# K of two units leaves PSUM by ScalarE instead of VectorE, in a fused infini-attention and token-mixer kernel

## Chip, cores, metric

One core of a Trainium2 chip. The metric is the device time of the core in microseconds (us); smaller is better. TensorE ("PE" in the profile) does the matmuls; their results land in PSUM, in eight banks, 0 to 7. VectorE ("DVE") and ScalarE ("ACT") take them out of PSUM into SBUF, the on-chip memory for everything else, and GpSimd ("POOL") applies the causal mask there.

## The reference, cut to what matters

```python
xn = layernorm(x)                               # x: 1 x 2048 x 1024
out = x + A(xn, wq, wk, wv, wo, beta) + B(xn, w1, b1, w2, b2)

def A(x, ...):                                  # 32 heads of 32, 4 segments of 512 tokens
    phi = lambda t: where(t > 0, t + 1.0, exp(t))
    M, z = 0, 0
    for s in range(4):
        qs, ks, vs = ...                        # projections of this segment
        p = softmax(qs @ ks.T * scale + causal_mask)
        a_dot = p @ vs
        a_mem = (phi(qs) @ M) / (phi(qs) @ z + 1e-06)
        outs.append(g * a_mem + (1.0 - g) * a_dot)
        M, z = M + phi(ks).T @ vs, z + sum(phi(ks))
    return concat(outs) @ wo

def B(x, ...):                                  # mixes tokens: two matmuls with gelu between
    ...
```

## The kernel before, the parts that matter

The mixer B comes first; attention begins near 374 us, with the projections, and near 388 us with the logits. Attention is cut into 32 **units**: unit u is a group of four heads in segment u // 8. While unit u's logits are made, dense jobs (eight matmuls of 512 columns each, into PSUM bank 6 or 7 by turns) project Q and K of unit u + 2, project V and apply wo. K of units 0 to 15 is projected here and leaves PSUM by a VectorE cast; K of later units is loaded from memory, where an earlier part of the kernel has put it.

```python
def q_job(self, u):                     # ends in: ScalarE copies the bank to qT (line 1253)
    ...
def k_job(self, u):
    def end(b):
        fw, k = self.fw, u % 3
        fw.op("dve", lambda e: e.tensor_copy(self.kT[k][:], self.bank(b)),        # line 1262
              reads=[self.R_bank[b]], writes=[self.R_kT[k]])
        if u // N_GRP < N_SEG - 1:
            self.exps.append((1, self.kT[k], self.R_kT[k], u))   # exp(K), later, on ScalarE
    return self.proj_job(self.wk_ring, u, end)
```

The weighted values of a unit are made in three parts. Parts 0 and 2 share bank 4, part 1 has bank 5; VectorE takes each out by an addition into `ost`. So part 2 can't start before the addition of part 0 is done:

```python
def weigh(self, u, part):
    ...
    b = 4 + part % 2
    ...                                         # matmuls into bank b
        fw.op("dve", lambda e: e.tensor_tensor(dst, src, eps, op=ALU.add),        # line 1418
              reads=[self.R_bank[b], self.R_eps], writes=[self.R_ost[o][part]])
```

The order in which a unit's work is given out (cut; `dense(n)` is n matmuls of the waiting jobs; `self.side` is VectorE work that is slipped in between them):

```python
for u in range(N_UNIT):
    self.jobs.extend(self.unit_jobs(u))         # ..., Q of u + 2, K of u + 2 (last)
    self.dense(cuts[0]);  self.logits(u, 0)     # banks 0 to 3, then Exp on ScalarE, mask on GpSimd
    self.dense(cuts[1])
    self.weigh(u - 1, 0);  self.dense(cuts[2], False)
    self.weigh(u - 1, 1);  self.dense(cuts[3], False)
    self.weigh(u - 1, 2)
    ...                                         # side: combine (u - 1), phi of Q, then:
    if u + 1 < N_UNIT:
        self.side.append(lambda u=u: (self.phi_k(u + 1), self.k_transpose(u + 1)))
    self.dense(cuts[4]);  self.logits(u, 1)
    ...                                         # even u: logits step 2; then the rest of the jobs
```

Thus the end of round 11 puts into VectorE's queue, in this order, phi of K of unit 12 (the last of the side work), the cast of K of unit 13 (the last job), and, from the next round, the addition of part 0 of unit 11. Round 13 does the same two units later.

## Time and profile before

| | before |
|---|---|
| time, 3 runs | 652.3 us median (652.26 to 652.78) |
| TensorE busy | 645.9 us, 99% of the 650.5 us span |
| K's casts on VectorE | 16, 688 ns each |
| first Q matmul of unit 13 to part 2 of unit 11 ("stretch A") | 477.19 to 483.91: 6.72 us |
| first Q matmul of unit 15 to part 2 of unit 13 ("stretch B") | 496.45 to 503.18: 6.73 us |
| from there to the start of VectorE's last addition to the output ("rest") | to 648.30: 145.12 us |

A run's time varies by some tenths of a microsecond from its start-up and its loads, long before the changed instructions. The stretches begin and end within the trace of one run, so they leave that out. They follow TensorE, which is never long idle; between the end of A and the start of B lie 12.52 to 12.55 us in every kernel here.

The groups of instructions by line, for the two ways of taking a 512-column bank out of PSUM (line, engine, operation, output from input, shapes, count; then busy us and mean ns of one; then idle time before and its releaser):

```profile
L1253 ACT ACTIVATE qT<-ps_all 128x512 bf16<-128x512 f32 x32 | 19.0, 594 | 23.3 <-PE ps_all L199 23.3
L1262 DVE CAST kT<-ps_all 128x512 bf16<-128x512 f32 x16 | 11.0, 688 | 12.9 <-PE ps_all L199 12.9
```

The two engines need about the same time for it. VectorE's timeline at the end of round 11 has that queue (start and length in us, then engine, line and operation as above; in other lines a bracket at the end gives the engine's idle time just before and what ended it):

```profile
482.70 0.68 DVE L1262 CAST kT<-ps_all 128x512 bf16<-128x512 f32 x1
483.30 1.03 DVE L1418 TENSOR_TENSOR ost<-ps_all,eps 128x396 bf16<-128x396 f32 x2
```

The addition starts 0.60 us after the cast, though the cast is 0.68 long: neighbours on VectorE overlap a little. TensorE's timeline and the chain for the same moment are in the prediction.

### The profile page before, as it was taken

What the parts mean: (1) busy time and instruction counts of PE and PEld (TensorE: products, weight loads), DVE (VectorE), ACT (ScalarE), POOL (GpSimd) and SP (SyncE); (2) the same over time, 40 slices, a digit from 0 to 9 for tenths busy, and PEclk for the clock granted to TensorE, in tenths of its full rate; (3) what the DMA queues carried; (4) which work ended last, traced back from release to release, by engine and by line L of the source; (5) the groups of instructions that cost most, each with busy time, mean ns of one, the idle gap of its engine ahead of it and who ended that gap; (6) DMA issues with size and microseconds to landing.
All of it is one profiled execution on the core that took longest, in us unless ns stands there. A gap on an engine that the chain in (4) does not pass through costs nothing.

```text
span 650.5 us, 11182 instructions
## 1 busy us (share of the span) xinstructions
PE 645.9 (99%) x4611; PEld 303.6 (47%) x4611; DVE 433.7 (67%) x808; ACT 281.4 (43%) x305; POOL 154.2 (24%) x179
## 2 busy tenths in 40 slices
PE   9999999999999999999999999999999999999998
PEld 3444444444444444444444444444544454445544
DVE  6975676665555664744638325767887888777896
ACT  7543232232210000111101047778767778889770
POOL 2500000000011220220202203343334444554440
PEclk9999999999999999999999999999999999999999
DMA  9804233242498947538262957979654677435434
GB/s 303 216 0 130 65 107 88 64 116 79 127 261 193 238 120 210 157 102 231 79 208 96 263 130 177 184 168 227 134 135 98 155 165 139 112 98 128 105 94 139
DMA packets 190123, 95.00 MB, mean 146 GB/s; under 512 B 108664, under 2 KB 176248, under 8 KB 190072
## 3 DMA queue, kind: packets, MB, share of 16 engines
q1 hardware_dynamic: 189928, 94.25, 57.2%
q8 instruction: 36, 0.59, 0.4%
q14 instruction: 15, 0.12, 0.1%
q10 hardware_dynamic: 144, 0.03, 0.0%
HBM read 69.23 MB, written 11.53 MB: 124 GB/s over the span
## 4 chain that ended last, share of the span: by engine, by line
PE 94%; DVE 3%; ACT 2%; issue 1%; DMA 0%; POOL 0%; DVEq 0%
PE ps_all L199 94%; ACT pT L1364 1%; DVE prod L1465 1%; DVE ln_st L587 1%; DMA xin<-in_A_x_dram 0%; DVE h L627 0%; DVE ost L1418 0%; POOL ln_rs L611 0%; DVE mtmp L1230 0%; DVE kT L1262 0%; DVE fin L1307 0%; DVE mtmp L1228 0%; ACT qT L1253 0%; ACT vA L1293 0%; DVE ln_mv L590 0%
## 5 line engine op out<-in xcount | busy, mean ns | idle before, releaser
L1364 ACT ACTIVATE pT<-ps_all 128x2048 bf16<-128x2048 f32 x80 | 150.2, 1877 | 47.4 <-PE ps_all L199 46.9
L1368 POOL TENSOR_SCALAR_AFFINE_SELECT pT<-pT 128x512 bf16<-128x512 bf16 x128 | 105.6, 843 | 160.7 <-ACT pT L1364 160.7
L689 DVE TENSOR_TENSOR part<-ps_all,part 128x512 f32<-128x512 f32 x84 | 57.7, 690 | 108.2 <-PE ps_all L199 87.8
L1075 POOL TENSOR_TENSOR part<-part,stg 128x512 f32<-128x512 f32 x24 | 33.0, 1404 | 285.1 <-DVE part L689 285.1
L199 PE MATMUL ps_all<-wv,xnT 128*128 128x512 bf16 x256 | 68.5, 380 | 0.4 <-ACT qT L1253 0.2
L746 ACT ACTIVATE g<-part,b1c 128x512 f16<-128x512 f32 x36 | 26.0, 722 | 98.8 <-DVE part L689 98.8
L199 PE MATMUL ps_all<-xnT,wq 128*128 128x512 bf16 x256 | 66.4, 380 | 0.0
L199 PE MATMUL ps_all<-wo,oT 128*128 128x512 bf16 (+2 forms) x272 | 63.8, 367 | 0.0
L694 ACT ACTIVATE part<-ps_all 128x512 f32<-128x512 f32 x24 | 14.0, 596 | 101.1 <-PE ps_all L199 67.1
L1418 DVE TENSOR_TENSOR ost<-ps_all,eps 128x396 bf16<-128x396 f32 (+1 forms) x72 | 37.2, 522 | 28.5 <-PE ps_all L199 27.8
L199 PEld LDWEIGHTS ps_all<-vA,pT 128*128 128x128 bf16 x1280 | 45.7, 96 | 20.4 <-DVE ost L1418 1.7
L199 PE MATMUL ps_all<-g,sum 128*128 128x512 f16 x224 | 51.0, 379 | 0.0
L199 PE MATMUL ps_all<-g,w2s 128*128 128x512 f16 x224 | 51.0, 379 | 0.0
L199 PE MATMUL ps_all<-gT,sum 128*128 128x512 f16 x224 | 50.3, 379 | 0.0
L199 PE MATMUL ps_all<-vA,pT 128*128 128x33 bf16 x1280 | 48.5, 177 | 0.3 <-DVE ost L1418 0.3
L199 PE MATMUL ps_all<-h,sum 128*128 128x512 f16 x192 | 45.2, 379 | 0.0
L199 PE MATMUL ps_all<-h,w1s 128*128 128x512 f16 x192 | 44.9, 379 | 0.0
L199 PE MATMUL ps_all<-hT,sum 128*128 128x512 f16 x192 | 43.6, 379 | 0.0
L199 PEld LDWEIGHTS ps_all<-wo,oT 128*128 128x128 bf16 x272 | 23.9, 98 | 24.4 <-issue 3.7
L199 PEld LDWEIGHTS ps_all<-xnT,wq 128*128 128x128 bf16 x256 | 22.6, 97 | 25.4 <-issue 5.3
L199 PEld LDWEIGHTS ps_all<-g,sum 128*128 128x128 f16 x224 | 21.9, 98 | 26.4
L199 PEld LDWEIGHTS ps_all<-g,w2s 128*128 128x128 bf16 x224 | 21.9, 98 | 26.4
(118 smaller groups left out, 875.1 us busy)
## 6 DMA issues: line engine op xcount, KB each, us to landing
w2s<-in_B_w_dram SPq DMA_DIRECT2D x8, 1792.0 KB, 9.5
w1s<-in_B_w_dram SPq DMA_DIRECT2D x12, 1024.0 KB, 5.6
wq<-in_A_wq_dram SPq DMA_DIRECT2D x32, 256.0 KB, 3.3
xs<-in_A_x_dram SPq DMA_DIRECT2D x24, 256.0 KB, 3.4
stg<-in_A_x_dram SPq DMA_DIRECT2D x16, 256.0 KB, 2.9
out_dram<-stg SPq DMA_DIRECT2D x16, 256.0 KB, 3.9
wk<-in_A_wk_dram SPq DMA_DIRECT2D x16, 256.0 KB, 3.6
fin<-out_dram SPq DMA_DIRECT2D x16, 256.0 KB, 3.2
```

The costliest lines, as they stand in the source:

```text
L199: ins = self.nc.tensor.matmul(*args, **kwargs)
L587: fw.op("dve", lambda e: e.bn_stats(st[:, 6 * h:6 * h + 6], src[:, 512 * h:512 * h + 512]), reads=[self.R_xin[c]], writes=[R])
L689: self.fw.op("dve", lambda e: e.tensor_tensor(self.tmp[dst][:], self.bank(b), self.tmp[src][:], op=ALU.add), reads=[self.R_bank[b], self.R ...
L694: self.fw.op("act", lambda e: e.activation(self.tmp[dst][:], self.bank(b), ACT.Copy), reads=[self.R_bank[b]], writes=[self.R_tmp[dst]])
L746: self.fw.op("act", lambda e: e.activation(self.gB[f % 2][half][:, f // 2, :], src, ACT.Gelu_apprx_tanh, bias=self.b1c[:, f:f + 1], scale= ...
L1075: fw.op("pool", lambda e: e.tensor_tensor(self.tmp[t][:], self.tmp[t][:], self.stg[k][:, 512 * half:512 * half + 512], op=ALU.add), reads= ...
L1364: fw.op("act", lambda e: e.activation(dst, src, ACT.Exp, scale=SCALE), reads=self.R_bank[0:4], writes=[R[v % 2][kb] for v, kb, _ in blocks ...
L1368: fw.op("pool", lambda e: e.affine_select(d, d, pattern=[[0, 4], [1, P]], compare_op=ALU.is_ge, fill=0.0, base=0, channel_multiplier=-1), ...
L1418: fw.op("dve", lambda e: e.tensor_tensor(dst, src, eps, op=ALU.add), reads=[self.R_bank[b], self.R_eps], writes=[self.R_ost[o][part]])
L1465: fw.op("dve", lambda e: e.tensor_tensor(self.prod[:], ost[:, :, 0:D_HEAD], rec.unsqueeze(2).to_broadcast([P, 32, D_HEAD]), op=ALU.mult), ...
```

## The change

Intent: two of K's casts stand in front of an addition that TensorE waits for; ScalarE is idle at that moment, so it takes these two.

```diff
+    K_BY_ACT = (13, 15)
+
     def k_job(self, u):
         def end(b):
             fw, k = self.fw, u % 3
-            fw.op("dve", lambda e: e.tensor_copy(self.kT[k][:], self.bank(b)),
-                  reads=[self.R_bank[b]], writes=[self.R_kT[k]])
+            if u in self.K_BY_ACT:
+                fw.op("act", lambda e: e.activation(self.kT[k][:], self.bank(b), ACT.Copy),
+                      reads=[self.R_bank[b]], writes=[self.R_kT[k]])
+            else:
+                fw.op("dve", lambda e: e.tensor_copy(self.kT[k][:], self.bank(b)),
+                      reads=[self.R_bank[b]], writes=[self.R_kT[k]])
             if u // N_GRP < N_SEG - 1:
```

## The prediction

> **What bounds the kernel now.** I read the page's shares first, then the chain that ended last in order of time, then each engine's timeline around the two places that the change touches. The page says who carries the time:
>
> ```profile
> PE 645.9 (99%) x4611; PEld 303.6 (47%) x4611; DVE 433.7 (67%) x808; ACT 281.4 (43%) x305; POOL 154.2 (24%) x179
> PE 94%; DVE 3%; ACT 2%; issue 1%; DMA 0%; POOL 0%; DVEq 0%
> ```
>
> The first line is busy time by engine, the second the chain's shares. TensorE is busy 99% of the 650.5 us span and makes 94% of the chain. VectorE's 67% is therefore no bound on average; it can cost time only where TensorE stands still for it. A change on VectorE and ScalarE can win only what TensorE loses to waits. So I looked in the chain for K's eviction (line 1262) and found it twice (start in us, length in us, what):
>
> ```profile
> 482.09 0.69 DVE mtmp L1230
> 482.78 0.60 DVE kT L1262
> 483.38 0.49 DVE ost L1418
> 483.87 0.05 issue
> 483.91 11.86 PE ps_all L199 x127
> ...
> 501.36 0.69 DVE mtmp L1230
> 502.05 0.60 DVE kT L1262
> 502.65 0.49 DVE ost L1418
> 503.14 0.05 issue
> 503.18 42.96 PE ps_all L199 x485
> ```
>
> These are exactly units 13 and 15. K is evicted 16 times, in order of units, and the timeline of VectorE has the last three casts at 482.70, 490.87 and 501.96 us: units 13, 14, 15. Unit 14's isn't in the chain. Each time the chain passes through VectorE's queue: phi of K, then the cast of K, then the addition that takes part 0 of the weighted values (ost) out of bank 4, and only then TensorE may write part 2 into bank 4. The timeline of TensorE shows the hole:
>
> ```profile
> 482.75 0.22 PE L199 MATMUL ps_all<-MZbf,pqT 128*128 128x132 bf16 x1
> 483.17 0.59 PE L199 MATMUL ps_all<-wv,xnT 128*128 128x512 bf16 x2
> 483.91 0.57 PE L199 MATMUL ps_all<-vA,pT 128*128 128x33 bf16 x16 [0.16 <-DVE ost L1418]
> ...
> 502.00 1.02 PE L199 MATMUL ps_all<-wv,xnT 128*128 128x512 bf16 x4
> 503.18 0.57 PE L199 MATMUL ps_all<-vA,pT 128*128 128x33 bf16 x16 [0.16 <-DVE ost L1418]
> ```
>
> The bracket's 0.16 us counts from the modelled end of the last matmul, and matmuls overlap, so it understates the loss. I count starts instead. Where nothing waits, two matmuls of 512 columns take 0.43 us from start to start of what follows (482.32 to 482.75) and four take 0.86 (548.74 to 549.60, same operands, no wait). So TensorE wanted to start at 483.17 + 0.43 = 483.60 and at 502.00 + 0.86 = 502.86. It lost 483.91 - 483.60 = 0.31 us and 503.18 - 502.86 = 0.32 us, 0.63 us together, under 0.1% of the time. That is the whole prize; these are also the only two waits that the timeline marks before a matmul from 450 to 510 us.
>
> **What the Trainium skill says.** "VectorE: DVE Perf Modes", section on the TRN2 errata, gives a VectorE move from PSUM to SBUF 120 + N cycles at 0.96 GHz; for fp32 (no fast mode from PSUM) and N = 512 I work that out as 658 ns. The trace has 688 for the casts of line 1262, of which about 0.60 us is what each holds the queue (482.70 to 483.30). "ScalarE: Activation LUTs", section "What ACT_TABLE_LOAD costs", gives 186 ns + 0.833 ns per element with immediate scale and bias, 613 ns here, and an overlap of about 93 ns between instructions back to back. The same copy is in the trace as Q's eviction: 594 ns mean over 32, and an exponential starts 0.49 us after one (488.71 to 489.20), an overlap of 0.11. The same page, "Table sets: the hidden batching unit", says that copy is in every table set; the trace agrees: copies and exponentials alternate all through attention, and there are just two table loads (lines 506 and 1004), both earlier. "SBUF — State Buffer", "Who interferes with whom", says that a VectorE instruction with two SBUF inputs contends with a GpSimd one that reads SBUF. The trace fits: prod takes 1.22 us alone and 1.66 at 479.42, beside a POOL mask that runs from 479.25 to 481.57. The cast reads only PSUM, so taking it away should not alter that contention by itself.
>
> **The change part by part.** Removed: two of VectorE's 16 casts, 2 x 0.60 us of its queue. In the chain, both lie right in front of the addition that TensorE waits for. Without it, the addition follows phi of K at 482.70 instead of 483.30 (its input, part 0 in bank 4, was done by about 482.5) and ends at 483.30 + 0.57 - 0.60 = 483.27; TensorE wants the bank at 483.60. Margin 0.33 us, far above the 0.04 that TensorE needs after the addition. At unit 15: 501.96 + 0.57 = 502.53 against 502.86, the same margin. So 0.60 us less of queue buys not 0.60 but only the 0.31 and 0.32 that TensorE lost.
>
> Added: two copies on ScalarE, about 2 x 0.59 us. K's last matmul ends at 478.93 + 1.89 = 480.82. ScalarE is idle then:
>
> ```profile
> 479.12 0.60 ACT L1253 ACTIVATE qT<-ps_all 128x512 bf16<-128x512 f32 x1
> 481.19 1.88 ACT L1364 ACTIVATE pT<-ps_all 128x2048 bf16<-128x2048 f32 x1 [1.47 <-PE ps_all L199]
> ...
> 500.46 1.88 ACT L1364 ACTIVATE pT<-ps_all 128x2048 bf16<-128x2048 f32 x1 [1.47 <-PE ps_all L199]
> ```
>
> The copy runs from about 480.85, so the exponential behind it starts at 480.85 + 0.49 = 481.34 instead of 481.19: 0.15 us late. Behind it come the exponentials of Q and K and the V eviction, all 0.15 us later. Does that reach TensorE? The next logits rewrite banks 0 to 3 at 485.15 - 0.31 = 484.84, and this exponential ends near 483.22: 1.6 us to spare. The next exponential must start at 485.60 - 0.31 = 485.29, and ScalarE is free at 484.01 + 0.15 + 0.49 = 484.65. At unit 15 it is closer: free at 503.27 + 0.15 + 0.49 = 503.91, needed at 504.43 - 0.32 = 504.11, 0.20 us to spare. Hidden both times. K's exponential still finds its input: it starts 2.6 us after K's matmuls end, and now on the same engine.
>
> Moved: nothing in the order of TensorE's work, since the flag that puts VectorE's side work into the dense jobs stays as it is. The bank of K comes free about 1.9 us earlier, but its next user (wo at 484.62) came 1.2 us after the old cast's end at 483.38, so that buys nothing.
>
> Sum: 652.3 - 0.31 - 0.32 = 651.67 us.
>
> **The rivals.**
> 1. Another wait takes the place of this one, gain 0, 652.3 us. Part 2 needs, besides bank 4, the masked pT (POOL done at 481.57), pqT (VectorE done at 479.51), the transposed K (issued at 474.25, 3 us to land) and the state of a segment earlier. All are ready at least 2 us before 483.60, so I see nothing that could replace it.
> 2. ScalarE becomes the bound after unit 15, where only 0.20 us is spare. If its copy cost 0.3 us more than I think, the gain would halve: 652.0. Against it: ScalarE idles 0.57 to 1.47 us before the exponentials that wait for logits here.
> 3. The gain is lost again later. From 503.18 the chain is TensorE for 43 us; then near 550 and 580 it passes through ScalarE for some 5 us. Those stretches begin with logits from TensorE (550.84, 580.80, each released by PE), so they move along with it, and no DMA stands in the chain after the start. Had one paced it, 652.3.
> 4. The full 2 x 0.60 us of the chain's kT pieces is won: 651.1. The chain's length of a piece isn't its worth: TensorE has work up to 483.60 and 502.86 whatever VectorE does. I hold this for very unlikely, unless the earlier addition helps something that I don't see.
>
> **Range and chances.** The mechanism is marked in the chain, both margins are 0.3 us, and later parts hang on TensorE, so I take the full 0.63 us: 651.7 us. The three runs of before spread over 0.5 us (652.26 to 652.78), nearly as much as the effect, and rivals 1 to 3 lie within 0.6 us above. So 651.2 to 652.4. Two per cent is 13 us, eleven times the 1.2 us by which all of VectorE's removed work could shorten anything: within 2% 0.98, and 0.01 each for faster and slower.
>
> **What would show it right or wrong.** In the profile after: the two waits of TensorE on ost near 483.9 and 503.2 are gone, part 2 follows its dense matmuls after 0.43 and 0.86 us; kT has 14 casts on VectorE and two copies near 594 ns on ScalarE, each with the exponential 0.49 us behind its start; VectorE about 1.4 us less busy, ScalarE 1.2 more; work past 510 us comes 0.6 us earlier with the same spacing, to the end. I am wrong if part 2 still waits (for POOL, a DMA or the second addition), if a wait of TensorE on pT appears near 506, or if the 0.6 us at 510 us has shrunk by the end.

## More of the kernel before

The framework waits for every producer that an instruction needs, in the order in which they were found (this order matters in one experiment):

```python
def _waits(self, es, reads, writes, extra=()):
    need = {}
    ...
    for t in need.values():
        es.wait_tok(t)
```

## The result, and the profile after

After: 651.63 us median of 6 runs (651.51 to 652.13). Before, in the same rounds: 652.36 (652.19 to 652.78, 6 runs). Ratio 0.9989, 95% interval 0.9977 to 1.0002. Here and below, a ratio is the mean time of one kernel's runs over that of the other's of the same rounds, so it isn't quite the ratio of the medians quoted. The medians differ by 0.73 us, with 0.6 us of spread within each kernel. The interval includes 1, so the total times alone would not prove a gain. The trace does.

The page's shares after, to be held against the first two lines of the prediction:

```profile
PE 646.1 (99%) x4611; PEld 304.0 (47%) x4611; DVE 432.7 (67%) x806; ACT 282.3 (43%) x307; POOL 153.8 (24%) x179
PE 94%; ACT 2%; DMA 2%; DVE 1%; issue 0%; POOL 0%; SPq 0%; DVEq 0%
```

VectorE has two instructions fewer and ScalarE two more. VectorE's share of the chain fell from 3% to 1%: the chain no longer passes through its queue before 484 and 503, where it held about 6 us each time. The 2% of DMA come from the chain's early part, which in this run went through a load that ended later (below). TensorE's timeline at the two places, to be held against the prediction's:

```profile
483.67 0.59 PE L199 MATMUL ps_all<-wv,xnT 128*128 128x512 bf16 x2
484.10 0.56 PE L199 MATMUL ps_all<-vA,pT 128*128 128x33 bf16 x16
...
502.17 1.02 PE L199 MATMUL ps_all<-wv,xnT 128*128 128x512 bf16 x4
503.03 0.56 PE L199 MATMUL ps_all<-vA,pT 128*128 128x33 bf16 x16
```

Both brackets are gone. Part 2 follows its dense matmuls after 484.10 - 483.67 = 0.43 us and 503.03 - 502.17 = 0.86 us. VectorE's timeline shows why: phi of K is followed at once by the addition.

```profile
482.59 0.69 DVE L1230 SCALAR_TENSOR_TENSOR mtmp<-kT,mtmp 128x512 bf16<-128x512 bf16 x1
483.20 1.23 DVE L1424 TENSOR_TENSOR ost<-ps_all,eps 128x396 bf16<-128x396 f32 x2
```

ScalarE's timeline, at unit 13 and at unit 15:

```profile
481.36 0.60 ACT L1265 ACTIVATE kT<-ps_all 128x512 bf16<-128x512 f32 x1 [1.13 <-PE ps_all L199]
481.85 1.87 ACT L1370 ACTIVATE pT<-ps_all 128x2048 bf16<-128x2048 f32 x1
...
503.58 0.60 ACT L1299 ACTIVATE vA<-ps_all 128x512 bf16<-128x512 f32 x1
504.27 1.88 ACT L1370 ACTIVATE pT<-ps_all 128x2048 bf16<-128x2048 f32 x1
```

The new copy stands in what was idle time (1.13 us were still idle before it) and delays the exponential behind it, which starts 0.49 us after the copy. The debt is paid at the next gap: after the V copy at 503.58 ScalarE would be free at 503.58 + 0.49 = 504.07, and the exponential starts at 504.27 because its logits end at 504.22, not because ScalarE was late.

The chain of waits, in order of time, no longer goes through VectorE near 484 and 503:

```profile
170.29 8.25 DMA w2s<-in_B_w_dram
...
388.45 1.89 ACT pT L1370
390.38 155.60 PE ps_all L199 x1696
546.00 4.65 PE ps_all L199 x70
```

Before, it left TensorE twice in this range for VectorE (the prediction shows those lines); now TensorE runs from 390 to beyond 550 us with no other engine in between.

The stretches: A 6.41 us (was 6.72), B 6.40 (was 6.73), rest 145.11 (was 145.12). So 0.31 + 0.33 = 0.64 us were won, and none was lost afterwards.

One thing in this trace invites a wrong reading. The work past 510 us is only about 0.17 us earlier than before in absolute time (555.56 against 555.73 for the same V matmul). But the profiled run was the slowest of the six (652.13). It was already 0.31 us later than the one before at 159 us, and 0.50 later at the first VectorE sum behind the w2 load (178.57 against 178.07). The changed instructions run 300 us later; this is the load's and the start-up's spread between runs.

### The profile page after: what moved, and what is told of

It is laid out like the page before. It is cut to its first block, busy times and chain, and to the rows that moved or that the text cites. A ratio compares the mean times of both kernels' runs of the same rounds, so it can differ in the third digit from the quotient of the medians. Undisturbed runs are those within 1.5% of the kernel's fastest.

```text
span 650.4 us, 11182 instructions
## 1 busy us (share of the span) xinstructions
PE 646.1 (99%) x4611; PEld 304.0 (47%) x4611; DVE 432.7 (67%) x806; ACT 282.3 (43%) x307; POOL 153.8 (24%) x179
## 4 chain that ended last, share of the span: by engine, by line
PE 94%; ACT 2%; DMA 2%; DVE 1%; issue 0%; POOL 0%; SPq 0%; DVEq 0%
PE ps_all L199 94%; ACT pT L1370 1%; DMA w2s<-in_B_w_dram 1%; DMA xin<-in_A_x_dram 1%; DVE sum L648 0%; DVE ln_st L587 0%; DVE h L627 0%; ACT junk L600 0%; POOL ln_rs L611 0%; DVE part L689 0%; ACT junk L597 0%; ACT qT L1253 0%; ACT vA L1299 0%; DVE gT L663 0%; DVE ln_mv L609 0%
## 5 line engine op out<-in xcount | busy, mean ns | idle before, releaser
L199 PEld LDWEIGHTS ps_all<-gT,sum 128*128 128x128 f16 x224 | 21.9, 98 | 26.7 <-DVE gT L663 0.6
```

Of the source, the lines that this page charges most:

```text
L199: ins = self.nc.tensor.matmul(*args, **kwargs)
```

## The experiments

Theory: at two places TensorE stands 0.31 to 0.33 us before part 2, because the addition of part 0 stands behind a cast in VectorE's queue; what is won is exactly that standing time. Rivals: VectorE's total load counts (then any cast moved would do, and all of them would bring more); the copy on ScalarE costs something back; the gain is lost again later. Medians of the kernel before were 652.29, 652.26 and 652.38 us (9 runs each) in the three groups of runs (first to fourth, fifth to eighth, ninth to twelfth experiment).

| kernel | A | B | rest | time, median (range) | ratio [95%] |
|---|---|---|---|---|---|
| before | 6.72 | 6.73 | 145.12 | see above | 1 |
| the change | 6.41 | 6.40 | 145.11 | 651.63 (651.51 to 652.13) | 0.9989 [0.9977, 1.0002] |
| e1_only13 | 6.41 | 6.73 | 145.13 | 651.93 (651.81 to 652.44) | 0.9996 [0.9983, 1.0010] |
| e2_only15 | 6.73 | 6.40 | 145.13 | 652.12 (651.89 to 652.15) | 0.9996 [0.9984, 1.0009] |
| e3_even | 6.73 | 6.73 | 145.14 | 652.46 (652.24 to 653.42) | 1.0005 [0.9993, 1.0018] |
| e4_act_extra | 6.73 | 6.72 | 145.14 | 652.32 (652.25 to 652.57) | 1.0001 [0.9989, 1.0014] |
| e5_double | 7.46 | 7.45 | 145.14 | 653.77 (653.67 to 654.26) | 1.0024 [1.0012, 1.0037] |
| e6_phi_later | 6.40 | 6.40 | 145.78 | 652.25 (652.18 to 652.35) | 0.9999 [0.9986, 1.0013] |
| e7_all | 6.41 | 6.40 | 145.13 | 651.49 (651.46 to 651.67) | 0.9988 [0.9976, 1.0001] |
| e8_q_dve | 6.40 | 6.41 | 144.94 | 651.46 (651.28 to 651.61) | 0.9987 [0.9975, 1.0000] |
| e9_phi_later_first | 6.40 | 6.73 | 145.15 | 652.15 (651.88 to 652.36) | 0.9996 [0.9983, 1.0009] |
| e10_q_dve_order | 6.40 | 6.40 | 144.65 | 651.19 (651.14 to 651.41) | 0.9982 [0.9970, 0.9995] |
| e11_qv_dve_order | 6.41 | 6.40 | 144.78 | 651.35 (651.25 to 651.44) | 0.9984 [0.9970, 0.9997] |
| e12_after_again | 6.41 | 6.40 | 145.12 | 651.67 (651.65 to 651.93) | 0.9990 [0.9977, 1.0003] |

All in us; all correct; all within 2% of before. Each experiment has 5 runs. Between kernels that don't differ there, A and B repeat to 0.01 us and the rest to 0.04.

### e1_only13 and e2_only15: one unit at a time

```diff
-    K_BY_ACT = (13, 15)
+    K_BY_ACT = (13,)        # e1;  (15,) in e2
```

> K of unit 13 alone by ScalarE. I measure two stretches of TensorE in the profile: A from the first Q matmul of unit 13 to part 2 of unit 11 (6.72 us before, 6.41 after the change), B from the first Q matmul of unit 15 to part 2 of unit 13 (6.73 before, 6.40 after), and the rest from that part 2 to the last addition of the output (145.12 before, 145.11 after). Queue theory (only the addition behind the cast in VectorE's queue held TensorE): A 6.41, B 6.73, rest 145.1, time 0.3 us under before. Rival, total load of VectorE (any 0.6 us taken from it helps a little everywhere): A and B in between, rest shorter.

> K of unit 15 alone by ScalarE. Queue theory: A 6.72, B 6.40, rest 145.1, time 0.3 us under before; with e1 the two gains add to that of the change. Rival, the second wait exists only because the first put TensorE out of step: then B would be 6.40 in e1 too, and e2 would gain nothing.

Measured: each shortens its own stretch (6.41 and 6.40) and leaves the other at 6.73. From TensorE's timeline, in e1 the only wait marked at the two places:

```profile
502.74 0.57 PE L199 MATMUL ps_all<-vA,pT 128*128 128x33 bf16 x16 [0.16 <-DVE ost L1424]
```

and in e2:

```profile
484.06 0.58 PE L199 MATMUL ps_all<-vA,pT 128*128 128x33 bf16 x16 [0.16 <-DVE ost L1424]
```

So the two halves are independent and add up: 0.31 + 0.33.

### e3_even and e7_all: other casts

```diff
-    K_BY_ACT = (13, 15)
+    K_BY_ACT = (12, 14)              # e3;  tuple(range(2, 16)) in e7
```

> K of units 12 and 14 by ScalarE, 13 and 15 back on VectorE: as much moved, in units where VectorE is idle for over 2 us after the cast. Queue theory: A 6.72, B 6.73, rest 145.1, time as before within 0.15 us. Rival, load of VectorE, or ScalarE being the better engine for such a copy: about 0.6 us under before as in the change.

> K of units 2 to 15 by ScalarE. Queue theory: the other twelve casts held TensorE nowhere that the profile marks, so A 6.41, B 6.40 and the time is that of the change or up to 0.2 us off it, unless ScalarE comes late in the first segment, where it is busier. Load theory: 0.3 us for each cast moved, 4 us under before.

Measured: e3 takes as much load off VectorE as the change does, and wins nothing in any stretch (its time is 0.17 us above before's, with one outlier of 653.42). e7 takes off twelve casts more than the change, and its stretches are the change's to 0.02 us. VectorE's load as such isn't what counts; only the casts of units 13 and 15, with an addition behind them that TensorE waits for, bring anything.

### e4_act_extra: ScalarE's share of the change alone

In before, ScalarE copies the bank too, into a buffer that the later exponential overwrites; VectorE's cast stays:

```diff
     def end(b):
+        if u in (13, 15):
+            fw.op("act", lambda e: e.activation(self.etmp[2 * (u % 2) + 1][:], self.bank(b), ACT.Copy),
+                  reads=[self.R_bank[b]], writes=[self.R_etmp[2 * (u % 2) + 1]])
         fw.op("dve", lambda e: e.tensor_copy(self.kT[k][:], self.bank(b)), ...)
```

> The copies on ScalarE as an addition: K of units 13 and 15 is copied by ScalarE into a buffer that is overwritten right after, and VectorE's cast stays where it was. Queue theory: ScalarE's exponential after it starts 0.15 us later, TensorE does not see it: A 6.72, B 6.73, rest 145.1, time as before within 0.15 us. Rival, ScalarE's copy costs something that the change hides in its gain: A or B longer than before by up to 0.15 us, or a wait of TensorE on pT near 506 us.

Measured: 6.73, 6.72, 145.14, and 652.32 against 652.29. The two copies on ScalarE cost nothing here. TensorE is some 0.3 us late in this kernel anyway, so that a smaller cost could hide behind it; that the change itself has none is seen in its own stretches, where the full 0.31 and 0.33 are won and the rest is 145.11. Together they refute that ScalarE pays for the change.

### e5_double: the suspected cost twice

The cast of units 13 and 15 is given out twice, onto the same tile:

```diff
         fw.op("dve", lambda e: e.tensor_copy(self.kT[k][:], self.bank(b)), ...)
+        if u in (13, 15):
+            fw.op("dve", lambda e: e.tensor_copy(self.kT[k][:], self.bank(b)), ...)
```

> VectorE casts K of units 13 and 15 twice, one right behind the other. Queue theory: the addition comes 0.60 us later than before, so both holes grow by 0.60: A 7.32, B 7.33, rest 145.1, time 1.2 us over before. Rival, VectorE has slack and the hole comes from elsewhere (bank, POOL): A and B stay near 6.72.

Measured: A and B grew by 0.74 and 0.72, where I had put 0.60 each. VectorE's timeline, and TensorE's wait:

```profile
482.68 0.69 DVE L1262 CAST kT<-ps_all 128x512 bf16<-128x512 f32 x1
483.40 0.69 DVE L1265 CAST kT<-ps_all 128x512 bf16<-128x512 f32 x1
484.01 1.04 DVE L1421 TENSOR_TENSOR ost<-ps_all,eps 128x396 bf16<-128x396 f32 x2
```

```profile
484.63 0.58 PE L199 MATMUL ps_all<-vA,pT 128*128 128x33 bf16 x16 [0.89 <-DVE ost L1421]
```

The second cast starts 0.72 us after the first, 0.03 after its end, because it writes the same tile and waits on VectorE's own semaphore for it. The addition behind it depends on no cast and follows after 0.61, before the cast's end. So my doubling added a wait of 0.12 that the original doesn't have; the edit was not clean in that respect. The point stands: once the queue is later than TensorE wants, each further 0.72 us of it costs TensorE all of 0.72 (time +1.51 in the medians). The way back is not symmetric: taking 0.60 away wins only the 0.31 to 0.33 by which it was late.

### e6_phi_later: reorder the queue instead of moving work

K stays on VectorE everywhere. Phi of K of units 12 and 14, which stood in front of the casts, goes behind the addition of part 0:

```diff
+            if u - 1 in (11, 13):                 # right after self.weigh(u - 1, 0)
+                self.phi_k(u)
+                self.k_transpose(u)
...
-            if u + 1 < N_UNIT:
+            if u + 1 < N_UNIT and u not in (11, 13):
                 self.side.append(lambda u=u: (self.phi_k(u + 1), self.k_transpose(u + 1)))
```

> K stays on VectorE in all units; instead the phi of K of units 12 and 14 (0.93 us of VectorE's queue), which runs right before that cast, comes after the addition that takes part 0 of the weighted values out. Nothing is added on ScalarE. Queue theory: the addition comes 0.9 us earlier, A 6.41, B 6.40 as in the change, time 0.6 us under before. Rival, the gain came from K leaving its bank and being ready 2 us earlier by ScalarE: A 6.72, B 6.73, time as before.

Measured: both waits are gone (A 6.40, B 6.40), as expected, and still the time is before's: 652.25 against 652.26. (The rival, K's earlier release, isn't quite excluded by e6 alone, since VectorE's cast of unit 13 starts 0.94 us earlier too, at 481.76 instead of 482.70. But already before, the bank's next user came 1.24 us after the cast's end, so it had nothing to gain from it.) The rest has grown by 0.66. The expectation failed. The whole gain of both places is given back at one point, 5.7 us after part 2 of unit 13. TensorE there in e6:

```profile
508.23 1.25 PE L199 MATMUL ps_all<-wv,xnT 128*128 128x512 bf16 x5 [0.54 <-DVE fin L1307]
```

These matmuls take the bank that VectorE's addition `fin` (wo's result added to the output) empties. `prod` in front of it multiplies the weighted values by their scales. VectorE in e6:

```profile
505.91 1.65 DVE L1465 TENSOR_TENSOR prod<-ost,srec 128x1024 bf16<-128x1024 bf16 x1
507.49 0.68 DVE L1307 TENSOR_TENSOR fin<-ps_all,fin 128x512 bf16<-128x512 f32 x1
```

VectorE with the change:

```profile
506.22 1.22 DVE L1471 TENSOR_TENSOR prod<-ost,srec 128x1024 bf16<-128x1024 bf16 x1
507.36 0.68 DVE L1313 TENSOR_TENSOR fin<-ps_all,fin 128x512 bf16<-128x512 f32 x1
```

With the change, those matmuls start at 508.10, which is 5.07 us after part 2 (503.03); in e6 508.23 - 502.50 = 5.73. The 0.66 has two parts. First, the work was moved and not removed, so VectorE reaches its tail later: the update of the memory starts 503.97 - 502.50 = 1.47 us after part 2, against 504.27 - 503.03 = 1.24 with the change, 0.23 late. Second, `prod` takes 1.65 us instead of 1.22, 0.43 more. Beside it runs GpSimd's mask. First e6, then the change (each line is two masks):

```profile
505.69 2.38 POOL L1368 TENSOR_SCALAR_AFFINE_SELECT pT<-pT 128x512 bf16<-128x512 bf16 x2 [3.00 <-ACT pT L1364]
...
506.21 2.31 POOL L1374 TENSOR_SCALAR_AFFINE_SELECT pT<-pT 128x512 bf16<-128x512 bf16 x2 [2.86 <-ACT pT L1370]
```

With the change the first mask starts at 506.21, together with `prod` (506.22), and it is the mask that becomes long: 1.72 us, where one with no such neighbour takes 0.64. In e6 the first mask starts at 505.69, 0.22 us ahead of `prod`, and takes 0.81, so it still runs 0.59 us beside `prod`, which loses 0.43. Elsewhere `prod` loses 0.44 where the mask still runs 0.58 (before, 479.42), 0.31 where it runs 0.45 (after, 487.89) and 0.10 where it runs 0.24 (e9, 487.74). The Trainium skill, "SBUF — State Buffer", section "Who interferes with whom", has just this: a VectorE instruction with two SBUF inputs contends with a GpSimd instruction that reads SBUF, and the order of issue decides which of them is blocked. The trace agrees. TensorE and with it the logits, the exponential and the mask had come 0.53 us earlier, VectorE's `prod` only 0.31, and so their order flipped. 0.23 + 0.43 = 0.66. All of it reaches TensorE, because there is no slack at this point: with the change, too, the matmuls start only 0.06 us after `fin` ends (508.10 after 507.36 + 0.68 = 508.04), just as in e6 (508.23 after 508.17).

### e9_phi_later_first: the same at one place

If e6 failed because the moved work lies as a debt in front of a point without slack, then moving phi only at unit 12, where VectorE has 2.25 us idle after the unit to pay it, must win (edit against e6):

```diff
-            if u - 1 in (11, 13):
+            if u == 12:
...
-            if u + 1 < N_UNIT and u not in (11, 13):
+            if u + 1 < N_UNIT and u != 11:
```

> As e6, but only the phi of K of unit 12 comes later; that of unit 14 stays. In e6 both holes were gone (A and B 6.40) and the time came back at 508.23 us, where TensorE waited 0.54 us for VectorE's addition of the output (rest 145.78 instead of 145.11): after unit 13 VectorE has no idle time until then, while after unit 11 it idles 2.25 us. Debt theory: A 6.41, B 6.73, rest 145.1, time 0.3 us under before. Rival, late phi costs something by itself wherever it is: no gain, or the stretch from part 2 of unit 11 to the first Q matmul of unit 15 longer than 12.53.

Measured: A 6.40, B 6.73, rest 145.15, time 652.15 against 652.38. A's gain is kept. The debt belongs to the second place alone, where VectorE isn't idle between its tail and `fin`.

### e8_q_dve and e10_q_dve_order: the opposite move, later

From unit 16 on VectorE has no casts of K, and ScalarE is the busier helper. With the change, TensorE waits a little for ScalarE's copy of Q, as its timeline shows:

```profile
555.56 0.59 PE L199 MATMUL ps_all<-wv,xnT 128*128 128x512 bf16 x2 [0.18 <-ACT qT L1253]
```

So e8 is the change with, in addition, Q of units 22 and 26 by VectorE:

```diff
+    Q_BY_DVE = (22, 26)
     def q_job(self, u):
         def end(b):
-            fw.op("act", lambda e: e.activation(self.qT[k][:], self.bank(b), ACT.Copy), ...)
+            if u in self.Q_BY_DVE:
+                fw.op("dve", lambda e: e.tensor_copy(self.qT[k][:], self.bank(b)), ...)
+            else:
+                fw.op("act", lambda e: e.activation(self.qT[k][:], self.bank(b), ACT.Copy), ...)
```

> The change, and Q of units 22 and 26 by VectorE instead of ScalarE. The profile after the change has TensorE waiting for ScalarE's copy of Q at 555.56 (0.24 us by start to start) and 585.45 us (0.16). Same queue theory, other direction: both waits vanish, the rest is 144.7 instead of 145.1, time 0.4 us under the change. Rival, VectorE is the engine that is short there and work must not go to it: the rest 145.1 or longer.

Measured: rest 144.94, where I had expected 144.7. The two waits did go: from the start of the logits to the start of the V matmuls that waited are 0.38 and 0.33 us, instead of 0.57 and 0.49, 0.35 won together. But only 0.17 reached the end. In e8 the logits start later behind the exponential that empties their banks. ScalarE, then TensorE, in e8:

```profile
564.89 1.88 ACT L1376 ACTIVATE pT<-ps_all 128x2048 bf16<-128x2048 f32 x1 [0.87 <-PE ps_all L199]
```

```profile
566.91 0.40 PE L199 MATMUL ps_all<-qT,kT 32*128 32x256 bf16 x8
```

The exponential ends at 564.89 + 1.88 = 566.77 and the logits start 0.14 after. With the change, this gap is 0.05 at the same place (567.71 after 565.78 + 1.88 = 567.66). Moving Q's copy had changed the order in which TensorE's waits stand in the program: the wait for K's load came first and the one for ScalarE last. (With the change, too, the gap is 0.14 where the program has that order, as at 561.10 after 559.08 + 1.88 = 560.96.) e10 is e8 with the waits of TensorE sorted, from unit 18 on, so that those for loads come last:

```diff
-        for t in need.values():
+        order = list(need.values())
+        if es.name == "pe" and self.dma_last:        # set from unit 18 on
+            order.sort(key=lambda t: isinstance(t.key, tuple))
+        for t in order:
             es.wait_tok(t)
```

> As e8, and from unit 18 on TensorE's groups wait for compute engines first and for DMAs last. In e8 both waits for Q vanished, but half of the gain was lost at 566.91 and 596.16 us: there the logits started 0.14 us after the exponential's end instead of 0.05, and the only difference in their instructions is that the wait for ScalarE now came last, behind one for a DMA that was long done. Theory, a wait that is met last costs 0.08 us more when it is the last in the list: the rest falls from 144.94 to 144.75, and to 144.5 if the same holds at 560.22, 589.81 and near 618.5. Rival, the 0.08 has another cause (PSUM, VectorE's cast): rest stays 144.94.

Measured: rest 144.65, and 651.19 us against 652.38, ratio 0.9982. ScalarE and TensorE at the same place:

```profile
565.08 1.88 ACT L1380 ACTIVATE pT<-ps_all 128x2048 bf16<-128x2048 f32 x1 [0.87 <-PE ps_all L203]
```

```profile
567.01 0.40 PE L203 MATMUL ps_all<-qT,kT 32*128 32x256 bf16 x8
```

565.08 + 1.88 = 566.96, and the logits start 0.05 after. It is the best version here, with an interval that lies below 1 (e11's does, too). That the order is the cause is shown, since e10 and e8 differ in nothing else; why a wait that stands last costs 0.09 more isn't shown by any run.

### e11_qv_dve_order: one step further

V of one chunk each in rounds 21 and 25, where TensorE waits for ScalarE's copy, goes to VectorE too:

```diff
-            if m in (1, 2):
+            if m in (1, 2) or (m, c) in ((6, 1), (7, 1)):      # V by VectorE
```

> As e10, and V of two chunks (units 21 and 25) by VectorE, because TensorE waits for ScalarE's copy of V at 561.59 (0.16 us) and 591.17 (0.07) after the change. Queue theory: rest 0.2 us shorter than in e10, about 144.3, time about 0.8 us under the change. Rival, VectorE comes late for its additions there: rest as in e10 or longer.

Measured: rest 144.78 instead of the 144.3 expected, 0.13 worse than e10. The waits that I aimed at are gone (start to start 0.33 at 560.35 and 589.71), but TensorE has a new one:

```profile
591.57 0.25 PE L203 MATMUL ps_all<-vA,pT 128*128 128x33 bf16 x4 [0.28 <-POOL pT L1384]
```

This start comes 591.57 - 590.04 = 1.53 us after the V matmuls before it; in e10 it came after 1.09. It is the same neighbour as in e6, the other way round. The V cast pushed `prod` 0.48 us back (589.71, was 589.23), to where the mask starts (589.73, was 589.84). In e10 the mask came when `prod` was half done and took 1.10 us; in e11 it came right behind `prod`'s start and took 1.70, ending at 591.43, after the 591.13 at which TensorE wanted it. There are 0.09 us more lost near 563.72. This working comes from the traces; I made no further run to test it by itself.

### e12_after_again: the change once more

The changed kernel, unedited, beside the last three.

> The changed kernel once more, on the same chip as e9 to e11. A 6.41, B 6.40, rest 145.1 again to 0.03; its time 0.6 to 0.75 us under before.

Measured: 651.67 against 652.38, ratio 0.9990; A 6.41, B 6.40, rest 145.12. The gain of about 0.7 us in the medians repeats in a second set of runs.

## Why the prediction was right, point by point

The predicted 651.7 us stands against 651.63 (and 651.67 in e12), within the range. That the medians meet it to less than 0.1 us is in part luck, since one kernel's runs spread over 0.6 us; the stretches are the firm evidence.

- **The prize is TensorE's two holes.** Forecast 0.31 + 0.32, measured 0.31 + 0.33 in the stretches. Forecast spacings 0.43 and 0.86, measured the same. e1 and e2 show that each is its own, e3 and e7 that no other cast counts.
- **0.60 us less of queue buys only the lateness.** Right (rival 4, the full 1.2 us, is refuted); e5 shows that lateness added is paid in full.
- **ScalarE hides the copies.** Right: 597 ns each (forecast 594), the exponential 0.49 behind, 0.20 us to spare at unit 15 both forecast and measured, and e4 as the direct test. Rival 2 is refuted. Its estimate, that a copy 0.3 us longer would halve the gain, looks too pessimistic: the exponential of 504.27 ends at 506.15, and the logits that overwrite its banks start at 506.41, so that by these spacings a further 0.2 us would be hidden behind the 0.20. No run tests it.
- **No other wait steps in, nothing is lost later.** Right for this change (rest 145.11 against 145.12). Rivals 1 and 3 were not idle fears: e6 takes away the same two waits and loses everything at `fin`. What saves the change is that it takes work out of VectorE's queue where e6 only defers it. I had looked for slack on ScalarE and not for slack on VectorE behind part 2; had the change been a reordering, the prediction would have failed there.
- **Work past 510 us 0.6 us earlier.** True of the spacing, not of the absolute times of the profiled run (0.17), whose start-up was 0.5 us later. The check as I had put it was not sharp enough for an effect of this size.
- **Busy times.** VectorE fell by 1.0 us (forecast 1.4) and ScalarE rose by 0.9 (forecast 1.2). The removed and added instructions are right; other instructions' lengths vary by a few tenths in sum between runs.
- **"prod takes 1.22 us alone and 1.66 beside a POOL mask".** Too coarse. In the trace of before, too, a mask runs beside the `prod` of 506.38 (1.22 us): it started at the same time. `prod` is slow only where the mask was first, and by what the mask has left (figures under e6). It touched no number of the forecast, and it is much of what e6 failed on. It also hides another way to the same gain: the queue of before that ends in the late addition holds such a slow `prod` at both places (479.42 and 498.69, 1.66 us), and VectorE isn't idle from there to the addition. Its 0.44 us above 1.22 are more than the 0.31 and 0.32 that TensorE lost. By this estimate the cast is one of several pieces of the queue whose removal would close the holes; no run tries `prod`.

## What to carry to other kernels

Price the removal of a wait by the time that the bound engine stands still, counted from start to start, and not by the length of the instruction that you remove; then ask for slack on the engine that takes the work over. Work that is moved out of a queue helps; work that is moved back within it becomes a debt that has to meet idle time before the next point where the bound engine needs that engine. When an effect is as small as the spread of the runs, measure stretches within the trace, from one instruction of the bound engine to another, and test the change by parts.

## What the Trainium skill lacked or had wrong

- "VectorE: DVE Perf Modes", section on the TRN2 errata: its formula gives 658 ns for the fp32 cast of 512 columns from PSUM to SBUF. The runs show 688 (676 to 692), and 0.60 us from its start to that of an independent next instruction.
- "VectorE: DVE Perf Modes", section "The DRAIN you can't avoid": for a row of eight copies it finds that a semaphore after each costs nothing extra; it also says that an instruction that nothing holds starts earlier, without a size. In e5 the cast that waits for the one before starts 0.72 us after it; without such a wait 0.60 us lie between a cast's start and the next instruction's: 0.12 us for the wait.
- "ScalarE: Activation LUTs", section "What ACT_TABLE_LOAD costs": nearly right. It gives 613 ns for the copy and an overlap of 93 ns; the runs show 597 and 0.11 us.
- "SBUF — State Buffer", section "Who interferes with whom": agrees, and could have the sizes. `prod` takes 1.22 us, or 1.65 when a mask of 0.81 started 0.22 us ahead of it; the mask takes 0.64, or 1.10 to 1.72 when `prod` started ahead of it or together with it.
- No page that I read has this: the order in which a TensorE instruction's waits are programmed matters. Logits start 0.14 us after the exponential that they wait for when the wait for ScalarE stands last behind one for a load, and 0.05 when the waits for loads stand last; 0.29 us in the rest of the kernel (e8 against e10).
